# One weight load placed between the two halves of the first k and v loads, and its rounding done there

## The chip, the cores and the metric

The kernel runs on one core of one Trainium2 chip. The metric is the device time in microseconds of that core, the median of several executions. Before the change four executions took 1024.33 to 1025.48 us, with a median of 1025.05 us.

## The reference

The program is an attention without softmax, followed by a gated feed-forward block on its output.

```python
kv = np.einsum('bhsd,bhse->bhde', k, v)          # 8 batches, 8 heads, 576 x 64
out = np.einsum('bhsd,bhde->bhse', q, kv)
rms = np.sqrt(np.mean(out * out, axis=-1, keepdims=True) + 1e-06)
x = (out / rms * g_norm)                         # then (B,H,S,D) -> (B*S, H*D) = 4608 x 512
g = x @ w_gate                                   # 512 x 1536
silu = g * (1.0 / (1.0 + np.exp(-g)))
return (silu * (x @ w_val) @ w_out).astype(np.float32)
```

q, k, v and g_norm are float32. The three weight matrices are float64, so that each element is two 32-bit words; the kernel makes float32 values of them on the chip.

## The kernel before, in words

**Blocks.** The 4608 tokens are cut into nine blocks of 512. Each block has an attention part (class `Att`) and a feed-forward part (class `Ffn`). Block 0 is treated apart: its feed-forward part multiplies plainly, as soon as each weight piece is there (`plain_up`, L1009 to L1024), while later blocks use products with fewer multiplications (`Up`, `Inner`, `Down`). The change touches only what happens before and during block 0's `plain_up`.

**Start of block 0.** Four statements at L1060 to L1063 issue the loads: the first half of q (two transfers of 256 KB), k and v (`load_first_kv`), the second half of q, and the first four weight pieces. `load_first_kv` goes through two groups of four heads; each group has a large transfer of k and one of v on SyncE's queue (L230, 512 KB each) and a small one of each on ScalarE's queue (L233, 64 KB each). `first` then does the attention of block 0:

- `turn_q(0)` transposes q's first half on TensorE (L335), and ScalarE and VectorE copy the result out (L337, L339).
- `first_kv` multiplies k by v (L248): 36 small matmuls for the heads of the first group, and 36 for those of the second. ScalarE copies one bank (L252) and VectorE adds the other (L253, shown as its helper L111).
- `product` multiplies q by that (L355), squares on ScalarE (L366) and sums on VectorE (L367). It is done for both halves, with `turn_q(1)` between.
- `warm` issues seven 128x512 matmuls whose result nobody reads (L482).
- `root` and `scale` compute the reciprocal root and multiply (L373 to L392, the multiplication shown as helper L113); `turn_x` transposes the result (L402) and copies it into `x` on ScalarE (L403).

**Weight pieces.** There are 36 pieces of 512 KB, in the order w_gate 0, w_val 0, w_gate 1, ... and then w_out. Each is loaded into one of four `ld` buffers (L135), which q's two halves use too, and rounded by `Words`. `begin` (L139) is an Abs on ScalarE (L146) and three operations on VectorE (L147, L152, L153). `finish` (L157) is one activation on ScalarE (L160) and an addition on VectorE that writes the weight (L162). A ring of five buffers `r` holds the intermediate values, and q's and the attention's too.

**What sets the order.** The instructions are put on the engines' queues by a scheduler; `tc.issue_after` keeps an instruction from being placed before another. Each engine then works through its own queue in order. `weights(n)` (L1046) loads four pieces ahead and rounds up to piece n. In `first`, piece 0 is begun after the second half of q is copied (L466), between the two products, and finished after the scaling (L473). `weights(2)` follows at L1072, and then two pieces more for each step of `plain_up`.

Of the kernel before, what the change touches and what calls it, by code (L numbers as in the profile page):

```python
# [18 lines left out]
def kernel(  # L19
# [154 lines left out]
    words = {}  # L174

    def load_w(name, j):
        src = wviews[name][1]
        if name == "o":
            words[name, j] = Words(src[:, j : j + 1, :], (1,))
        else:  # L180
            words[name, j] = Words(src[:, :, 2 * P * j : 2 * P * (j + 1)], (NS,))

    def round_w(name, j):
        if name == "o":
            dst = wo[:, j : j + 1, :]
        else:
            dst = wviews[name][0][j // 2][:, :, P * (j % 2) : P * (j % 2 + 1)]
        piece = words.pop((name, j))
        if not piece.begun:
            piece.begin()  # L190
        return piece.finish(dst)

    class Att:
# [12 lines left out]
        def parts(self, t):  # L206

            n, first = self.n, P * t - D * self.n
            if t < self.cut:
                return [(n - 1, S + first, 0, P)]  # L210
            if t == self.cut and self.split:
                return [(n - 1, S - D, 0, D), (n, 0, D, P)]
            return [(n, first, 0, P)]
# [7 lines left out]
        def load_first_kv(self):  # L221


            room = self.room.rearrange("p f (h x) -> p (f h) x", h=2)
            most = {"k": room[:, 0:H], "v": room[:, H : 2 * H]}
            last = {x: room[:, 2 * H + i].rearrange("p (h d) -> p h d", d=D) for i, x in enumerate("kv")}
            for g in range(2):
                heads, rows = slice(NS * g, NS * (g + 1)), slice(D * g, D * (g + 1))
                for x, src in (("k", k), ("v", v)):
                    nc.sync.dma_start(  # L230
                        out=most[x][:, heads], in_=src[0, heads, 0:BLK].rearrange("h (p t) d -> p h (t d)", t=T)
                    )
                    nc.scalar.dma_start(out=last[x][rows], in_=src[0, heads, BLK:S].rearrange("h p d -> p h d"))  # L233
            self.k, self.v = (
                [most[x].rearrange("p h (t d) -> p h t d", t=T)[:, :, t] for t in range(T)] + [last[x]] for x in "kv"
            )
# [220 lines left out]

        def first(self):
            self.turn_q(0, (b_psum, c_psum))
            self.first_kv()  # L460
            self.product(0)
            with tc.issue_after(self.multiplied.ins):
                self.turn_q(1, (b_psum, c_psum))

            with tc.issue_after(self.copied_q.ins), tc.issue_after(self.summed.ins):
                begun = words[pieces[0]].begin()  # L466
            with tc.issue_after(begun.ins):
                self.product(1, (b_psum, a_psum))
            self.warm()
            self.root(0, 2)  # L470
            self.scale(0)
            with tc.issue_after(self.squared.ins), tc.issue_after(self.scaled.ins):
                weights(1)  # L473
            self.turn_x(0)
            self.scale(1)
            return self.squared, self.scaled
# [557 lines left out]
    pieces = [(x, j) for j in range(NF) for x in "gv"] + [("o", j) for j in range(NF)]  # L1034
# [3 lines left out]
    def load_weights(upto):  # L1038
        nonlocal loaded, sent
        while loaded < min(upto, len(pieces)):  # L1040
            load_w(*pieces[loaded])
            loaded += 1
            if loaded == len(pieces) - NP:
                sent = words[pieces[loaded - 1]].sent

    def weights(upto):  # L1046
        nonlocal rounded
        while rounded < min(upto, len(pieces)):
            load_weights(rounded + 4)
            round_w(*pieces[rounded])  # L1050
            rounded += 1

    def t2(place, b22, b11):

        sub(nc.vector, place, b22, place)
        add(nc.vector, place, place, b11)

    blocks = [Att(n) for n in range(NB)]
# [7 lines left out]
    for n in range(NB):  # L1066
        ffn = Ffn(n, blocks[n])
        nxt = blocks[n + 1] if n + 1 < NB else None
        if n == 0:

            with tc.issue_after(squared.ins), tc.issue_after(scaled.ins):
                weights(2)  # L1072
            ffn.plain_up(0, (0,))
            copied = blocks[0].copied
            blocks[0].turn_x(1)
            for f in range(NF):
                with tc.issue_after(blocks[0].copied.ins if f else copied.ins):
                    weights(2 * (f + 2))
                ffn.plain_up(f) if f else ffn.plain_up(0, (1,))
            weights(len(pieces))  # L1080
            pairs = wo.rearrange("p (j e) d -> p e j d", e=2)
            t2(pairs[:, 0, :, HD:DM], pairs[:, 1, :, HD:DM], pairs[:, 0, :, 0:HD])
            nxt.room = x_pool.tile([P, 3, 7, P], F32, name="xi").rearrange("p a b c -> p (a b c)")

            with tc.issue_after(sent.ins):
                for i in range(2):
                    nxt.load_kv(i)
                for i in range(2):
                    nxt.load_q(i)
            ffn.plain_end()  # L1090
            for g in range(2):
                nxt.kv(g)
        else:

            def third():
                nxt.kv(0)
                nxt.load_kv(1)

            def two_thirds():
                nxt.kv(1)  # L1100
                if nxt.n == 2:
                    for i in range(2):
                        nxt.load_q(i)

            fill = {4: third, 8: two_thirds} if nxt else {}
            if n == DEEP:
                for a, at in enumerate((1, 2, 3, 5)):
                    fill[at] = lambda i=a // 2, j=a % 2: nxt.load_quarters(i, (j,))
            ffn.up(fill)
        if nxt:  # L1110
            nxt.turn()
        if 0 < n < NB - 2:
            blocks[n + 2].load_kv(0)
        if DEEP <= n < NB - 2:
            for i in range(2):
                blocks[n + 2].load_q(i)
        ffn.down(nxt)
        if n == 0:
            blocks[2].load_kv(0)

            with tc.issue_after(nxt.halves[0].ins):
                for j in range(NP // 2):
                    t2(wv[j][:, 0:2], wv[j][:, 2:4], wg[j][:, 0:2])
            with tc.issue_after(ffn.down_.s4.ins):
                for j in range(NP // 2, NP):
                    t2(wv[j][:, 0:2], wv[j][:, 2:4], wg[j][:, 0:2])
# [31 lines left out]
```

## Time and profile before

| | |
|---|---|
| median of four runs | 1025.05 us (1024.33 to 1025.48) |
| profiled execution: its own time, its span | 1026.5 us, 1024.7 us |
| TensorE, VectorE, ScalarE, GpSimd busy, share of the span | 98%, 68%, 22%, 36% |
| mean transfer rate over the span; in the first 25.6 us | 166 GB/s; 216 GB/s |
| second half of the k-by-v products begins | 14.84 us |
| first full-width multiplication of the feed-forward part begins | 39.96 us |

The page lists the busy time of each engine, then the span in 40 slices of 25.6 us with the busy share of each in tenths. The chain of work that ended last is followed back from the last instruction: at each step to what released it, or to the instruction before it on its engine. In the timeline a row has the start, the length, the engine, the line, the operation, the tiles written and read, the shapes and how many instructions are merged; behind it, in brackets, the idle time of the engine just before and what ended it. SPq and ACTq are the queues that issue transfers. A transfer's length in the chain runs from its issue to its landing. A matmul of float32 values is recorded as two instructions, a transpose as one.

### The profile page before, as it was taken

The page shows a single profiled execution, that of the slowest core. Times are in us where ns is not written, and L with a number is a line of the kernel's source. Part 1 is how long each engine was busy: PE and PEld are TensorE (multiplying, and loading weights), DVE is VectorE, ACT ScalarE, POOL GpSimd, SP SyncE. Part 2 cuts the span into 40 slices and gives each one's busy share as a digit, 9 for nine tenths or more (in the row PEclk, how much of TensorE's full clock was granted, in tenths as well). Part 3 has the DMA queues.
Part 4 walks back from the last instruction along what each step waited for, and adds up shares of the span by engine and source line. Part 5 has one row for each costly group of instructions (what it writes and reads, how often), then busy time and mean ns, then how long its engine had stood idle before and what let it go on. Part 6 is the DMA issues. An engine that isn't in the chain of part 4 may idle for free.

```text
span 1024.7 us, 21404 instructions
## 1 busy us (share of the span) xinstructions
PE 1007.8 (98%) x8522; PEld 898.2 (88%) x8522; DVE 701.3 (68%) x1168; ACT 227.9 (22%) x352; POOL 368.9 (36%) x280
## 2 busy tenths in 40 slices
PE   5999999999999999999999999999999999999998
PEld 4544688888999989998999899988998999989997
DVE  2999688998666855685657566665669466956661
ACT  2666111221111212221121111111112111211110
POOL 0000263434045512561246314730555046413670
PEclk9999999999999999999999999999999999999999
DMA  7689644667888467845686468637762766066601
GB/s 216 198 256 268 122 82 128 170 153 173 243 224 239 79 154 207 253 102 116 212 240 151 83 203 244 186 56 199 231 195 54 177 196 187 21 164 207 190 28 42
DMA packets 273844, 170.26 MB, mean 166 GB/s; under 512 B 150608, under 2 KB 241872, under 8 KB 273744
## 3 DMA queue, kind: packets, MB, share of 16 engines
q1 hardware_dynamic: 238800, 164.42, 58.6%
q10 hardware_dynamic: 34880, 4.46, 2.7%
q8 instruction: 68, 1.11, 0.4%
q14 instruction: 32, 0.26, 0.1%
q0 software_dynamic: 64, 0.00, 0.0%
HBM read 138.02 MB, written 22.41 MB: 157 GB/s over the span
## 4 chain that ended last, share of the span: by engine, by line
PE 91%; DVE 5%; DMA 2%; issue 1%; ACT 1%; SPq 0%; DVEq 0%; ACTq 0%
PE b L714 26%; PE b L551 19%; PE c L714 13%; PE c L551 10%; PE a L714 6%; PE a L551 5%; PE b L1018 4%; PE c L1018 4%; PE m L314 2%; PE m L355 1%; DVE r L112 1%; DVE xi L112 1%; DMA h<-in_v_dram 1%; DVE r L111 1%; DVE t L112 1%
## 5 line engine op out<-in xcount | busy, mean ns | idle before, releaser
L111 POOL TENSOR_TENSOR r<-r 128x256 f32<-128x256 f32 (+1 forms) x105 | 110.8, 1061 | 301.1 <-DVE r L111 272.4
L111 DVE TENSOR_TENSOR r<-b,r 128x512 f32<-128x512 f32 (+1 forms) x273 | 162.0, 606 | 65.6 <-PE b L714 60.6
L112 POOL TENSOR_TENSOR t<-wo 128x512 f32<-128x512 f32 x81 | 114.4, 1436 | 214.9 <-DVE wo L111 105.8
L111 DVE TENSOR_TENSOR r<-c,r 128x512 f32<-128x512 f32 (+1 forms) x179 | 108.5, 617 | 87.9 <-PE c L714 54.5
L714 PE MATMUL b<-x,t 128*128 128x128 f32 x1092 | 151.2, 275 | 0.0
L111 DVE TENSOR_TENSOR r<-a,r 128x512 f32<-128x512 f32 (+1 forms) x99 | 62.5, 631 | 113.5 <-PE a L551 71.1
L714 PEld LDWEIGHTS b<-x,t 128*128 128x128 f32 x1092 | 136.5, 192 | 0.8 <-DVE r L111 0.2
L714 PE MATMUL c<-xi,t 128*128 128x128 f32 x840 | 112.4, 275 | 0.4 <-DVE xi L111 0.4
L113 POOL TENSOR_TENSOR h<-r 128x1024 f32<-128x1024 f32 (+1 forms) x40 | 82.2, 2068 | 78.1 <-DVE r L111 75.0
L714 PEld LDWEIGHTS c<-xi,t 128*128 128x128 f32 x840 | 102.9, 192 | 0.5 <-DVE xi L111 0.5
L551 PE MATMUL b<-wo,h 128*128 128x256 f32 x432 | 100.1, 383 | 0.1
L551 PE MATMUL b<-t,h 128*128 128x256 f32 x432 | 96.9, 381 | 0.0
L551 PEld LDWEIGHTS b<-t,h 128*128 128x128 f32 x432 | 81.5, 190 | 11.4 <-issue 0.2
L551 PEld LDWEIGHTS b<-wo,h 128*128 128x128 f32 x432 | 79.8, 190 | 13.2 <-DVE h L113 2.5
L728 ACT COPY r<-b 128x512 f32<-128x512 f32 x63 | 36.9, 586 | 211.5 <-PE b L714 211.5
L714 PE MATMUL b<-xi,t 128*128 128x128 f32 x588 | 79.7, 276 | 0.0
L714 PEld LDWEIGHTS b<-xi,t 128*128 128x128 f32 x588 | 72.4, 192 | 0.0
L714 PE MATMUL b<-x,wg 128*128 128x128 f32 x336 | 52.7, 279 | 0.2 <-DVE x L112 0.2
L714 PE MATMUL b<-x,wv 128*128 128x128 f32 x336 | 51.3, 275 | 0.0
L551 PE MATMUL a<-wo,h 128*128 128x256 f32 x216 | 48.3, 379 | 0.0
L551 PE MATMUL c<-t,s 128*128 128x256 f32 x216 | 48.1, 379 | 0.0
L551 PE MATMUL c<-wo,h 128*128 128x256 f32 x216 | 48.1, 379 | 0.0
(128 smaller groups left out, 1564.8 us busy)
## 6 DMA issues: line engine op xcount, KB each, us to landing
t<-w SPq DMA_DIRECT2D x336, 256.0 KB, 3.4
out_dram<-r SPq DMA_DIRECT2D x17, 512.0 KB, 3.1
ld<-in_k_dram SPq DMA_DIRECT2D x26, 288.0 KB, 4.9
ld<-in_v_dram SPq DMA_DIRECT2D x26, 288.0 KB, 5.9
ld<-in_moe_w_gate_dram SPq DMA_DIRECT2D x12, 512.0 KB, 4.8
ld<-in_moe_w_val_dram SPq DMA_DIRECT2D x12, 512.0 KB, 4.7
ld<-in_moe_w_out_dram SPq DMA_DIRECT2D x12, 512.0 KB, 4.9
w<-t SPq DMA_DIRECT2D x18, 256.0 KB, 3.3
```

The lines of the kernel that those rows point to most:

```text
L111: add = lambda e, o, a, b: e.tensor_tensor(out=o, in0=a, in1=b, op=OP.add)
L112: sub = lambda e, o, a, b: e.tensor_tensor(out=o, in0=a, in1=b, op=OP.subtract)
L113: mul = lambda e, o, a, b: e.tensor_tensor(out=o, in0=a, in1=b, op=OP.mult)
L314: nc.tensor.matmul(self.kv_ps[r][u * D : (u + 1) * D, g, :], lhsT=k[:, u, c, :], rhs=v[:, u, c, :], start=(c == 0), stop=(c == KT - 1),)
L355: self.multiplied = nc.tensor.matmul(self.ps[i][u][p : p + D, t, j, :], lhsT=self.qt[rows, 2 * i + t, j, p : p + D], rhs=kvs[b % 3][rows, ...
L551: nc.tensor.matmul(banks[e][:, e], lhsT=lhsT, rhs=rhs, start=first and i == 0 and (e == 0 or banks[0] is not banks[1]), stop=i == self.ste ...
L714: nc.tensor.matmul(ps[:, i, f], lhsT=self.weight(o, p, f), rhs=self.operand(o, p), start=first and (i, f) == (0, 0), stop=True, skip_group ...
L728: nc.scalar.copy(out=dst, in_=ps)
L1018: nc.tensor.matmul(t, lhsT=w[f // 2][:, i, P * (f % 2) : P * (f % 2 + 1)], rhs=x[:, i, of], start=(i == 0), stop=(i == NS - 1),)
```

## The change

The load of piece 0 (w_gate 0) is issued within `load_first_kv`, behind k and v of the first group of heads and ahead of those of the second; `load_weights(1)` has an effect only the first time that the loop reaches it. Piece 0 is rounded whole between `turn_q(0)` and `first_kv`. Where piece 0 was begun, piece 1 (w_val 0) is begun now, and each later call of `weights` reaches one piece further. The condition in `weights` asks whether q's second half has been asked for; it has been at every call.

```diff
@@ load_first_kv @@
                     nc.scalar.dma_start(out=last[x][rows], in_=src[0, heads, BLK:S].rearrange("h p d -> p h d"))
+                load_weights(1)
@@ first @@
             self.turn_q(0, (b_psum, c_psum))
+            weights(1)
             self.first_kv()
...
-                begun = words[pieces[0]].begin()
+                begun = words[pieces[1]].begin()
...
             with tc.issue_after(self.squared.ins), tc.issue_after(self.scaled.ins):
-                weights(1)
+                weights(2)
@@ weights @@
-            load_weights(rounded + 4)
+            load_weights(rounded + 4 if blocks[0].q[2:] else 1)
@@ block 0 @@
             with tc.issue_after(squared.ins), tc.issue_after(scaled.ins):
-                weights(2)
+                weights(3)
```

In the instructions as built, SyncE's queue differs from before in the place of this one load (it stands behind k and v of the first heads) and in two neighbouring transfers near 90 us. On TensorE the order differs only at the start of the feed-forward part. Before, it is: four matmuls with w_gate, seven transposes, four matmuls with w_val, one transpose. After, it is: one matmul with w_gate, four with w_val, four transposes, three with w_gate, four transposes. ScalarE's and VectorE's orders differ until all pieces are rounded, and are the same from then on. The load of w_val 1 takes the buffer that piece 0 has left, where before it took that of q's second half.

## Prediction

> **What bounds the kernel now.** I read the busy shares first, then the chain that ended last for the first 45 us, then the queue of SyncE and the other engines over the same stretch. From the page:
>
> ```profile
> PE 1007.8 (98%) x8522; PEld 898.2 (88%) x8522; DVE 701.3 (68%) x1168; ACT 227.9 (22%) x352; POOL 368.9 (36%) x280
> PE   5999999999999999999999999999999999999998
> ```
>
> TensorE is busy in all but the first slice of 25.6 us. So an edit at the start is worth what it does to the moment from which TensorE runs without a gap. The chain that ended last, in order of time (start, length, what):
>
> ```profile
> 5.22 9.48 DMA h<-in_v_dram
> 14.84 2.44 PE m L248 x72
> 17.37 0.43 DVE kv L111
> 17.85 1.99 PE m L355 x64
> ...
> 33.52 1.28 ACT L1023
> 34.81 0.39 ACT h L1023
> 35.20 0.57 ACT r L160
> 35.77 0.59 ACT x L403
> 36.36 0.04 issue
> 36.41 1.99 PE b L1018 x8
> 38.40 1.73 PE c L1018 x8
> 40.13 3.43 PE b L1018 x8
> ```
>
> Until 14.70 us the end hangs on a transfer, v of the second four heads. From 14.84 to 30 us it hangs on TensorE and the work of block 0's attention; from 31 to 36.4 on ScalarE; from 36.41 on TensorE alone: the chain holds nothing but L1018 from there to 115.66. What moves the start of the first full-width L1018 group, 39.96 us, moves the end; what lies beside that path costs nothing. The queues at the start, from the timeline (start, length, engine, operation):
>
> ```profile
> 4.81 0.37 SPq L230 DMA_DIRECT2D h<-in_k_dram  x1
> 5.22 1.14 SPq L230 DMA_DIRECT2D h<-in_v_dram  x1
> 6.46 5.13 SPq L298 DMA_DIRECT2D ld<-in_q_dram  x2
> 11.63 2.72 SPq L135 DMA_DIRECT2D ld<-in_moe_w_gate_dram  x1
> 11.75 2.40 PE L248 MATMUL m<-h 64*64 64x64 f32 x72 [4.69 <-DMA h<-in_v_dram]
> 14.84 2.41 PE L248 MATMUL m<-h 64*64 64x64 f32 x72 [0.69 <-DMA h<-in_v_dram]
> ...
> 31.26 1.99 PE L1018 MATMUL b<-x,wg 128*128 128x256 f32 x8 [0.34 <-ACT x L403]
> 33.09 0.69 DVE L162 CUSTOM_DVE_ANT_0 wv<-r 128x1024 uint16<-128x1024 uint16 x1
> 33.85 1.97 PE L1018 MATMUL c<-x,wv 128*128 128x256 f32 x8
> ```
>
> Both halves of L248 wait for v, the first until 11.75, the second until 14.84. The transfer queue is full in that time. The stretches' row (TensorE's, its loads', VectorE's, ScalarE's, GpSimd's busy time, clock, share of the 16 transfer engines, GB/s):
>
> ```profile
> 6.00:12.00 6.00, 1.31 (x13) 0.94 (x17) 0.23 (x1) 0.59 (x1) 0.00 (x0) 1.00 1.09 325
> ```
>
> **The change part by part.** Times below are those of the profiled execution: span 1024.7 us, its own time 1026.5 us, against a median of 1025.05 us of the four runs. I work out a difference from the profiled run and add it to the median.
>
> *The load, moved.* One issue of 512 KB goes on SP from behind k, v and the two q loads to a place ahead of k and v of the second heads: past four issues (k, v, q, q). The issue took 0.37 to 2.72 us of SP; at the new place SP is free at 4.81, so k is issued at about 5.2 instead of 4.81, v at about 6.5 instead of 5.22. Both still stand behind 1 MB that lands by 11.75, so issue time is not the price. The price is 512 KB ahead of k and v in a queue that serves in order. The two L248 groups give it: 1 MB (k and v of the second heads) between 11.75 and 14.84, 3.09 us, so 1.54 us per 512 KB. Other rows: 512 KB at 325 GB/s is 1.61 us; at the 216 GB/s that the page gives for the whole first slice it is 2.43 us. Nothing would be the lower end, if the transfer engines had room; their share of 1.09 in 6 to 12 us speaks against it. I take 1.54, the row of the same packets at the same place, and keep 0 and 2.43 for the range.
>
> DMA: Bandwidth & Descriptors (the Trainium skill), section Specifications, gives a limit of about 358 GB/s per core from HBM; 512 KB by it would be an estimated 1.46 us and the sum 0.08 us smaller. Its Rules for kernel authors say to issue a DMA early and wait on it late; here early means in front of transfers that the chain waits for, and the trace's rows decide against that rule.
>
> *What waits behind k and v.* L248's second half, the sum L111, the product L355, the q transposes, the second product, the warming L482, the root and scale: all of it moves by 1.54 us, since each hangs on the one before. q's second half stays behind v in the queue and lands 1.54 us after its new v at the latest as now; L335 at 19.77 started with no wait, and it moves too.
>
> *The first piece's rounding, moved.* On ScalarE the Abs (L146, 0.68 us) and the unit (L160, 0.67 us) now stand before and after the copy of the second q tile; on VectorE L152, L147, L153 and L162 (0.42, 0.43, 0.69, 0.68 us) stand before the sum L111. The Abs waits for the weight, about 11.75 + 1.54 = 13.3 us. Queued behind it on ScalarE: the q copy (at 7.10 now, needed by L355 at 19.4) and the kv copy (18.4); on VectorE: L111 at 18.9. ScalarE would be through at about 15.3, VectorE at 16.3. Cost nothing; the cover is the wait for k and v, and without it (weight landing with v at 16.2) VectorE would end near 18.9, still hardly late.
>
> *The begin at 22.25, replaced.* The Abs, the three VectorE operations and the L160 that stood there for piece 0 now stand there for piece 1 (w_val), same kinds and sizes. Piece 1 has the same bytes ahead of it as piece 0 and 1 had together; the transfer share falls to 0.15 by 20 to 21 us, so it is in by then, against a need at 22.25 + 1.54 = 23.8. Nothing.
>
> *The gap before 36.41.* With piece 1 finished at 30.0 (the L162 at 29.35) instead of 33.8, the order of TensorE changes: one matmul on wg, four on wv, four transposes, three on wg, four transposes, then the second half. ScalarE's order was L146, L160, L146, table load, Silu, L160, two copies of x (L403); it becomes L146, L160, copy, table load, Silu, copy. That is 1.7 us of rounding less to 0.57 + 0.58, but a copy that must wait for transposes stands ahead of the table load (1.28). Replayed without the shift: a matmul is two records, spaced 0.216 us at 256 columns; a transpose takes 0.109. The first wg matmul runs 31.26 to 31.79, the four on wv to 33.52, four transposes to 33.96 (the last result 0.2 later), their copy 34.16 to 34.84, the table load to 36.12, the Silu to about 36.4, the other copy to 37.09. TensorE's three wg matmuls and four transposes end at 35.69; the next half starts there, does two matmuls, waits from 36.55 to 37.15 for the other copy, and its wv part starts at 38.01 instead of 38.24. Gain 0.22 us. Bounds: 0, and TensorE's whole idle time between 29.88 and 39.96: 10.08 less 16 x 0.109 less 32 x 0.216 = 1.42 us. I take 0.22.
>
> *The fourth weight (w_val, second piece).* Its issue waited until 21.76 for L335 to free a q buffer; now it takes the buffer of piece 0 and goes out some 6 us earlier. It stands behind everything the chain needs. Later loads, and VectorE's order of roundings to 104.5 us, shift among themselves; L1018 has no wait for a weight in 36 to 115 us. Nothing, cover: the lead of the rounding, L162 of the piece for 43.40 ends at 37.9.
>
> *TensorE's clock.* Four 128-wide transposes took 1.11 us at 19.77 and eight took 1.04 at 29.88: the array doubles its speed between. The first warming half-step took 0.72 us, the next 0.43. If the doubling keeps its distance to the work, nothing; if it keeps its time, L482 gains 0.29; if it comes late, L482 at half speed (14 x 0.43 more) is the far bound, 6.0. I take 0, as nothing in the busy stretch from 17.85 on changes but its start.
>
> TensorE: Matmul & The Clock Gate (the Trainium skill), section Part 1, says that the full clock is granted after a busy window of about 3.4 us of a free-running count. Being a window late would make that an estimated 1.7 us at most; the added idle time of L248 (14.15 to 16.4) is shorter than a window.
>
> **Sum.** 1.54 - 0.22 = +1.3 us: 1026.4 us on the median, 1027.8 by the profiled run's own time. That is 0.13%, under the 0.2% (2.05 us) that I take as what a measurement of this kernel can tell from no change.
>
> **The rivals.**
> - *The transfer costs more.* At 216 GB/s it is 2.43, and the sum +2.2: 1027.3, slower by over 0.2%; it decides from a price of 2.27 us on. For it: the slice's mean, and the q packets that halve the rate to 193 GB/s in 12 to 16 us. Against: these lie behind v.
> - *The clock comes late.* L248's longer idle time and the shifted work delay the doubling. Each us more of half speed in L482 costs 0.5 us, and nothing hides it: L402 follows L482 (30.04), the scale is ready before (29.43). With 2 us of delay the sum is +2.3: 1027.4; from 1.5 us on it decides. For it: the doubling lies within 1 us of L482's start.
> - *The load hides.* k and v are not delayed, the gap closes: -0.2 to -1.4, 1023.6 to 1024.8, and with 0.6 from an earlier clock (30.04 down to the scale's 29.43) it just reaches 2 us. Against: the full queue.
> - *The weight does not go ahead*, so that only order changes: +-0.2. The changed kernel's order of instructions on SP rules it out, where the load stands fourth.
>
> **How the numbers follow.** Forecast (own range 1025.6 to 1027.1) 0.50; dear transfer 0.25; late clock 0.13; hidden load 0.12, half of it over 0.2%. Slower: 0.25 + 0.13 and 0.03 of the forecast's edge. Same: the rest of the forecast with half the hidden load. For 8 in 10 the range leaves out half of each end: 1024.4 to 1028.2, the upper end being dear transfer with half of a late clock.
>
> **What would show it.** In the changed kernel's profile: L248's second half starting at 16.4 (at 17.3 the transfer was dear; at 14.8 hidden); the Abs at about 13.3; L482 ending at 31.6; the table load ahead of the first full-width L1018, which starts at 41.3. The prediction is wrong if that start is not 1.3 us later, or if it is and the end is not: then a later stage gave or took time.

## The result, and the profile after

The changed kernel takes 1026.7 us (median of 30 runs, 1025.21 to 1028.92); the kernel before, run beside it, takes 1024.95 us (median of 48 runs, 1023.63 to 1026.22). The ratio is 1.0018, with a 95% interval of 1.0012 to 1.0023. That is +1.75 us, within +1.2 and +2.4: slower by an amount that the interval separates from zero. The middle value is just inside the 0.2% that the prediction counts as no change, the upper end of the interval is not. The forecast was +1.3 us on a median of 1025.05, so 1026.4 us.

The profiled executions differ by less than the medians: span 1024.7 us before, 1025.0 us after. The profiled execution before lies above its own median (1026.5 us against 1024.95), that of after on its own (1026.73 against 1026.7). So the difference of the two spans is not the effect of the change, and everything below is read as distances within one execution.

The page of the changed kernel, busy shares:

```profile
PE 1006.6 (98%) x8522; PEld 897.3 (88%) x8522; DVE 702.3 (69%) x1168; ACT 227.9 (22%) x352; POOL 368.8 (36%) x280
...
PE   5999999999999999999999999999999999999998
```

Hardly anything has changed there: TensorE still works without a gap after the first slice. So the first 41 us are compared, as in the prediction. The changed file has one more line from L234 on and two more from about L462 on, so L249, L336, L356, L403, L484 and L1020 below are what was L248, L335, L355, L402, L482 and L1018.

The timeline of the changed kernel at the start (start us, us, engine, line, operation, number merged, and in brackets the idle time before with what ended it):

```profile
4.51 0.37 SPq L135 DMA_DIRECT2D ld<-in_moe_w_gate_dram  x1
4.92 0.89 SPq L230 DMA_DIRECT2D h<-in_k_dram  x1
...
11.09 2.40 PE L249 MATMUL m<-h 64*64 64x64 f32 x72 [4.32 <-DMA h<-in_v_dram]
...
12.62 0.68 ACT L146 ACTIVATE r<-ld 128x512 f32<-128x512 f32 x1 [7.77 <-DMA ld<-in_moe_w_gate_dram]
...
14.64 0.69 DVE L162 CUSTOM_DVE_ANT_0 wg<-r 128x1024 uint16<-128x1024 uint16 x1
...
15.80 2.42 PE L249 MATMUL m<-h 64*64 64x64 f32 x72 [2.31 <-DMA h<-in_v_dram]
...
21.64 0.68 PE L336 MATMUL c<-ident,ld 128*128 128x128 f32 x4
```

The weight's issue now stands ahead of k and v of the second heads. The two groups of small products start 4.71 us apart (11.09 and 15.80), where they were 3.09 us apart, and the second waits 2.31 us for v instead of 0.69. The rounding of the weight (the Abs at 12.62, the last step at 14.64) is done before the second group starts. The transfer engines were as full as before in this time, and the rate was no higher:

```profile
6.00:12.00 6.00, 1.68 (x37) 1.30 (x37) 0.00 (x0) 0.00 (x0) 0.00 (x0) 1.00 1.06 316
```

The same timeline at the start of the feed-forward part:

```profile
30.27 1.06 PE L403 MATMUL m<-ident,r 128*128 128x128 f32 x8 [0.28 <-DVE r L113]
31.68 0.70 PE L1020 MATMUL b<-x,wg 128*128 128x256 f32 x2 [0.34 <-ACT x L404]
...
35.28 1.28 ACT L1025 ACT_TABLE_LOAD   x1
...
36.58 0.38 ACT L1025 ACTIVATE h<-b 128x256 f32<-128x256 f32 x1
36.86 0.68 ACT L404 ACTIVATE x<-m,gain 128x512 f32<-128x512 f32 x1
...
37.01 1.99 PE L1020 MATMUL b<-x,wg 128*128 128x256 f32 x8 [0.49 <-ACT h L1025]
...
40.57 3.60 PE L1020 MATMUL b<-x,wg 128*128 128x512 f32 x8
```

The same places before (the second four transposes, L402, and the first full-width groups with wg and with wv):

```profile
20.68 1.06 PE L335 MATMUL c<-ident,ld 128*128 128x128 f32 x4
...
29.88 1.04 PE L402 MATMUL m<-ident,r 128*128 128x128 f32 x8
...
39.96 3.60 PE L1018 MATMUL b<-x,wg 128*128 128x512 f32 x8
43.40 3.60 PE L1018 MATMUL c<-x,wv 128*128 128x512 f32 x8
```

The order of TensorE is the one that the built program showed. The second copy of x (L404 at 36.86) stands behind the table load and the Silu. From the first matmul on wg to the first full-width group it took 8.89 us (31.68 to 40.57), against 8.70 before. The second half on wg stood still for 0.49 us until the Silu (L1025) had read the first half.

**The sum of one execution.** The table gives distances in us; all but the last column are from the timelines. "g" are the starts of the two groups of small products, "q" the start of the product L355, "T" that of the transposes L402, "b" the first matmul with wg, "f" the first full-width group. The last column is how long after "q" TensorE's speed doubled, from the trace's record of its clock, which begins with the doubling (at 24.00 us before, at 21.79 after). Four of the experiments of the next section stand in it too.

| kernel | first g at | g to g | second g to q | q to T | T to b | b to f | first g to f | doubling after q |
|---|---|---|---|---|---|---|---|---|
| before | 11.75 | 3.09 | 3.01 | 12.03 | 1.38 | 8.70 | 28.21 | 6.15 |
| after | 11.09 | 4.71 | 3.01 | 11.46 | 1.41 | 8.89 | 29.48 | 2.98 |
| load alone | 11.84 | 4.79 | 3.02 | 12.02 | 1.38 | 8.71 | 29.92 | 6.13 |
| load behind | 10.52 | 3.02 | 3.02 | 12.08 | 1.37 | 8.90 | 28.39 | 6.24 |
| two loads | 10.98 | 6.28 | 3.01 | 11.73 | 1.40 | 8.90 | 31.32 | 4.06 |
| own bank | 11.90 | 4.68 | 3.02 | 11.83 | 1.38 | 8.61 | 29.52 | 5.65 |

After less before: +1.62 for the load, +0.03, +0.19 in the gap, and -0.57 between q and T: together +1.27 from the first group on. The first group itself started 0.66 us earlier, which gives the +0.61 by which the first full-width group is late (40.57 against 39.96). The last term and that earlier start are not the change's as far as these runs tell. The start of the first group lies between 10.52 and 11.90 us in these six profiles, with no order by kernel. The -0.57 is TensorE's clock: in the execution after, the second four transposes took 0.68 us (last line of the first timeline above), where they took 1.06 us in the other five. The whole distance q to T lies between 11.46 and 12.08 us in the six, and in all six the later the doubling, the longer it is. (The granted clock in the rows of the stretches is no help here: it reads 1.00 throughout this stage in all six, also ahead of the doubling.) Without those two, the load and the gap make +1.84 us with the 0.03, and the medians differ by 1.75.

Between the first full-width group and the end, the delay in this pair of executions goes from +0.61 to +0.23 us at the last matmul, most of it in one stretch at 224 to 243 us. From the start of that group to the start of the last matmul it is 981.06 us before and 980.68 after; with the load alone 980.25, with the load behind 981.12, with two loads 980.78, with the own bank 980.43, and 980.72 in the kernel before with early matmuls, which leaves the load where it was. The seven lie within 0.87 us, and two loads have no gain at 224 to 243 us. So nothing in these profiles lays this difference to the change, and no later stage adds to the loss.

### The profile page after: what moved, and what is told of

Its sections match the earlier page's. It is cut to its first block, busy times and chain, and to the rows that moved or that the text cites. A ratio compares the mean times of both kernels' runs of the same rounds, so it can differ in the third digit from the quotient of the medians.

```text
span 1025.0 us, 21403 instructions
## 1 busy us (share of the span) xinstructions
PE 1006.6 (98%) x8522; PEld 897.3 (88%) x8522; DVE 702.3 (69%) x1168; ACT 227.9 (22%) x352; POOL 368.8 (36%) x280
## 4 chain that ended last, share of the span: by engine, by line
PE 84%; DVE 9%; DMA 4%; SPq 1%; issue 1%; ACT 1%; ACTq 0%; DVEq 0%
PE b L716 26%; PE b L553 20%; PE c L716 13%; PE c L553 10%; PE a L716 6%; PE a L553 5%; DVE r L153 1%; PE m L356 1%; DMA h<-in_v_dram 1%; PE m L315 1%; SPq L283 1%; DVE xi L112 1%; DVE r L147 1%; DMA ld<-in_moe_w_out_dram 1%; DVE r L152 1%
## 5 line engine op out<-in xcount | busy, mean ns | idle before, releaser
L113 POOL TENSOR_TENSOR h<-r 128x1024 f32<-128x1024 f32 (+1 forms) x40 | 81.9, 2064 | 78.5 <-DVE r L111 75.0
```

Of the source, the lines that this page charges most:

```text
L113: mul = lambda e, o, a, b: e.tensor_tensor(out=o, in0=a, in1=b, op=OP.mult)
```

## The experiments

The theory: the 512 KB ahead of k and v cost their own transfer time on the path, some 1.6 us, and the new order in front of the second half costs 0.2 us more, because of the Silu. The rivals: the loss comes from the rounding that now stands between `turn_q(0)` and `first_kv`; it comes from a clock that doubles later; or it lies in a later stage.

### The load alone

Before, with the load moved and no rounding moved.

```diff
                     nc.scalar.dma_start(out=last[x][rows], in_=src[0, heads, BLK:S].rearrange("h p d -> p h d"))
+                load_weights(1)
```

> Only the load of piece 0 is moved, between the two groups of k and v; the rounding and every other order stay as before. If the queue is the cause, the second L248 group starts 4.6 to 4.8 us after the first (3.09 before) and the time is +1.5 to +1.7 us, about as much as the whole change (+1.75). If the cause is the new order of the rounding (the second half of the first feed-forward step waits for the Silu), the load alone is worth 0 to +0.5 us.

Measured: 1026.44 us (11 runs, 1025.54 to 1027.51) against 1024.98 us for before; ratio 1.0017 (1.0008 to 1.0026), so +1.46 us. Its timeline:

```profile
11.84 2.40 PE L249 MATMUL m<-h 64*64 64x64 f32 x72 [4.91 <-DMA h<-in_v_dram]
16.63 2.42 PE L249 MATMUL m<-h 64*64 64x64 f32 x72 [2.40 <-DMA h<-in_v_dram]
...
31.67 1.04 PE L403 MATMUL m<-ident,r 128*128 128x128 f32 x8
33.05 1.99 PE L1019 MATMUL b<-x,wg 128*128 128x256 f32 x8 [0.34 <-ACT x L404]
...
41.76 3.60 PE L1019 MATMUL b<-x,wg 128*128 128x512 f32 x8
```

The groups stand 4.79 us apart, 1.70 more than before, and every later distance is that of before within 0.01 us, the gap (8.71) among them. So the load alone makes nearly all of the loss, and the moved rounding is not needed for it. The distance is as expected; the time is just under the +1.5 to +1.7 us.

### The load behind k and v

The changed kernel with the load issued behind k and v of both groups and ahead of q's second half, and the rounding after `first_kv`.

```diff
@@ load_first_kv @@
-                load_weights(1)
+            load_weights(1)
@@ first @@
-            weights(1)
             self.first_kv()
+            with tc.issue_after(self.copied_kv.ins), tc.issue_after(self.added_kv.ins):
+                weights(1)
```

> The load stands behind both groups of k and v and ahead of q's second half, the rounding of piece 0 follows the sum of the k-by-v banks; everything behind is ordered as in the changed kernel. If the queue is the cause, the groups of L248 are 3.1 us apart again and the time is within -0.5 to +0.4 us of before. If the new order costs, it stays at +1.0 us or more.

Measured: 1025.50 us (11 runs, 1024.29 to 1027.0); ratio 1.0006 (0.9997 to 1.0015), +0.5 us, not told apart from no change. That is 0.1 us above the expected range, and the interval reaches to +1.5 us, so the time alone does not rule out the other expectation, +1.0 us or more. The distances do:

```profile
10.52 2.40 PE L249 MATMUL m<-h 64*64 64x64 f32 x72 [3.45 <-DMA h<-in_v_dram]
13.54 2.41 PE L249 MATMUL m<-h 64*64 64x64 f32 x72 [0.63 <-DMA h<-in_v_dram]
...
35.35 1.99 PE L1021 MATMUL b<-x,wg 128*128 128x256 f32 x8 [0.74 <-ACT h L1026]
```

The groups are 3.02 us apart again, the second group to q is 3.02 us as before, and the first group to the first full-width group 28.39 us against 28.21. The piece is still rounded early, and it brings no gain: the distance b to f is 8.90, as in the changed kernel, with a wait for the Silu again (0.74 us). So, together with the load alone, the place of the load made the loss, and not the early rounding.

### Two loads between

```diff
-                load_weights(1)
+                load_weights(2)
```

> The changed kernel with two weight pieces between the groups instead of one. If the queue is the cause, the groups are 6.2 to 6.4 us apart and the time is +3.0 to +3.6 us against before. If the transfer engines had room, or the order is the cause, it stays at about +1.8 us.

Measured: 1028.47 us (5 runs, 1027.25 to 1028.73); ratio 1.0033 (1.0020 to 1.0045), +3.5 us, as expected if the queue is the cause.

```profile
10.98 2.40 PE L249 MATMUL m<-h 64*64 64x64 f32 x72 [4.31 <-DMA h<-in_v_dram]
17.26 2.41 PE L249 MATMUL m<-h 64*64 64x64 f32 x72 [3.88 <-DMA h<-in_v_dram]
```

The groups are 6.28 us apart: 3.19 more than before for two loads, 1.60 each. No load, one load and two loads lie nearly on one line, 1.6 us per 512 KB. That is 328 GB/s, close to the rate at which the transfer engines ran in this stretch (305 to 325 GB/s in the rows of 6 to 12 us of the six kernels).

### A bank of its own for the second half

The changed kernel; the wg result of plain_up's second half goes to a new tile of the `b` ring, where it shared a tile with the first half that the Silu reads.

```diff
             if 0 in halves:
                 self.ps[f] = [pool.tile([P, 2, HB], F32, name=pool.name[0]) for pool in (b_psum, c_psum)]
+            elif f == 0:
+                self.ps[f][0] = b_psum.tile([P, 2, HB], F32, name="b")
```

> The changed kernel, but the second half of the first feed-forward step writes w_gate's product into a bank of its own, which the Silu of the first half doesn't read. If the wait for the Silu holds that half back, it now starts right behind the four transposes, waits for the second copy of x in its middle, and the step after it starts 0.3 to 0.4 us earlier counted from the first L1018: -0.3 us against the changed kernel. If the copy of x holds it, nothing moves.

Measured: 1026.80 us (11 runs, 1025.9 to 1027.85); ratio 1.0018 (1.0010 to 1.0027).

```profile
37.41 1.03 PE L1022 MATMUL b<-x,wg 128*128 128x256 f32 x4
37.71 0.38 ACT L1027 ACTIVATE h<-b 128x256 f32<-128x256 f32 x1
...
38.72 1.13 PE L1022 MATMUL b<-x,wg 128*128 128x256 f32 x4 [0.29 <-ACT x L404]
...
41.42 3.60 PE L1022 MATMUL b<-x,wg 128*128 128x512 f32 x8
```

The second half now starts at 37.41, before the Silu at 37.71, and then waits for the copy of x, as the prediction had replayed it. The distance b to f falls from 8.89 to 8.61 us, just under the expected 0.3 to 0.4. So the Silu's hold on the shared tile is what kept the gap from closing. In the median this 0.28 us doesn't show; it is less than these runs can tell.

### An earlier clock

A test of the clock's part, on the kernel before: four 128x512 matmuls whose result nobody reads, between `turn_q(0)` and `first_kv`. They are extra work and leave nothing out.

```diff
             self.turn_q(0, (b_psum, c_psum))
+            self.early(4)
...
+        def early(self, count):
+            ps = a_psum.tile([P, NS, P], F32, name="a")
+            for _ in range(count):
+                nc.tensor.matmul(ps, lhsT=ident, rhs=self.q[0], start=True, stop=True)
```

> The kernel before, with four more 128x512 matmuls that nobody reads between the transposes of q's first half and the k-by-v products, where TensorE waits for v. If the time to the first feed-forward step depends on when the array's speed doubles, the transposes of q's second half take 0.11 us each instead of 0.21 and the second product 1.1 us instead of 1.9, the scaling is ready near 26.6 us instead of 29.4, and the time is -2 to -3 us against before. If the wait for k and v alone sets it, -0.3 to +0.5 us.

Measured: 1027.02 us (10 runs, 1025.41 to 1028.12) against 1024.98; ratio 1.0021 (1.0011 to 1.0030), 2.0 us slower. The expectation was missed, sign included. The timeline of TensorE:

```profile
7.98 4.34 PE L483 MATMUL a<-ld,ident 128*128 128x512 f32 x7
12.25 1.38 PE L248 MATMUL m<-h 64*64 64x64 f32 x72
14.53 1.40 PE L248 MATMUL m<-h 64*64 64x64 f32 x72 [0.90 <-DMA h<-in_v_dram]
16.66 1.15 PE L355 MATMUL m<-kv,r 64*64 64x64 f32 x61 [0.73 <-DVE kv L111]
20.33 0.33 PE L355 MATMUL m<-kv,r 64*64 64x64 f32 x3 [2.53 <-issue]
20.59 1.12 PE L335 MATMUL b<-ident,ld 128*128 128x128 f32 x4
```

The clock did double early: each group took 1.38 to 1.40 us instead of 2.40. But in the middle of the next product TensorE stood still for 2.53 us and waited for nothing that the profile shows ("issue"). The stretches' rows (the last three columns are the granted clock, the share of the transfer engines and GB/s) show what that cost further:

```profile
18.00:19.00 1.00, 0.00 (x0) 0.00 (x0) 0.00 (x0) 0.00 (x0) 0.00 (x0) 1.00 1.00 335
...
21.00:22.00 1.00, 1.00 (x7) 1.00 (x6) 0.25 (x1) 0.72 (x2) 0.00 (x0) 0.50 0.06 16
...
24.00:25.00 1.00, 1.00 (x22) 0.66 (x15) 0.97 (x3) 0.63 (x2) 0.00 (x0) 1.00 0.93 302
```

The clock fell back to half from about 20.6 to 24 us, so that the transposes L335 and the second product ran slowly again. L335 began at 20.59, where it began at 19.77 before, although the second group had started 0.31 us sooner. The first full-width group is 0.87 us later than before if counted from the second group (25.99 against 25.12), so about 1.2 of the 2.0 us is not located by this profile. What held TensorE is not settled. It stopped behind the 61st of the product's 64 recorded matmuls, and at the same place, for 1.67 us, in the next kernel, with the same early matmuls. The transfer engines were full in the first half of the stall. The trace has a packet of 16 KB of the queue that the profile's page calls "instruction" in transfer at that time: from 18.12 to 19.09 us here (stall 17.81 to 20.33), from 16.11 to 17.32 in the next kernel (stall 17.14 to 18.81). That TensorE's own instructions came late would fit, but no run took it apart.

### Everything together

The changed kernel with the load behind k and v, the bank of its own, the four early matmuls, piece 1 begun only after the second product, and five warming matmuls instead of seven: an attempt at a version that beats both. The parts that have not been shown yet:

```diff
-            with tc.issue_after(self.copied_q.ins), tc.issue_after(self.summed.ins):
-                begun = words[pieces[1]].begin()
-            with tc.issue_after(begun.ins):
-                self.product(1, (b_psum, a_psum))
+            self.product(1, (b_psum, a_psum))
...
-            for _ in range(7):
+            for _ in range(5):
```

> The early matmuls; the load of piece 0 behind both groups of k and v, its rounding behind the sum of the banks; no begin of piece 1 ahead of the second product; five warming matmuls instead of seven; w_gate's second half in a bank of its own. The begin took 1.4 us of VectorE between the two sums of squares, so the scaling should be ready near 25.3 us: -3 to -4.3 us against before. If the begin was hidden behind TensorE, no better than the early matmuls alone.

Measured: 1024.75 us (11 runs, 1023.66 to 1025.97) against 1024.98; ratio 0.9998 (0.9989 to 1.0006). The expectation was missed. L403 began at 28.38, 1.50 us before that of the kernel before. The first full-width group with wg (40.18) is no mark here, because one of its four matmuls now runs ahead of wv's second half. The first full-width group with wv begins at 42.75, where it began at 43.40 before; counted from the second group of small products that is 28.88 us against 28.56, so nothing was won on the path.

The single runs show one more thing. In seven of the eleven, the profiled one among them, the mean granted clock was 0.996 to 0.998, and they took 1024.41 to 1025.97 us; the profile has the clock at half speed from 20.4 to 23.8 us. In the other four it was 1.00, and they took 1023.66 to 1023.93 us, all below the fastest of the 26 runs of the kernel before (1024.14). In the experiment ahead of this one, too, the one run at 1.00 was the fastest of the ten (1025.41). So the fallen clock goes with the longer times. This is a sorting of runs after the fact; no run made the clock stay up.

### The same without the early matmuls

The last kernel without `early(4)`.

> The same without the early matmuls. -1.0 to -1.8 us against before if VectorE's 1.4 us and the two warming matmuls were on the path; about 0 if the late doubling of the array's speed takes it back.

Measured: 1025.14 us (11 runs, 1024.42 to 1025.73); ratio 1.0003 (0.9994 to 1.0012). Missed too. The rows of TensorE and ScalarE in its timeline:

```profile
28.57 1.06 PE L403 MATMUL m<-ident,r 128*128 128x128 f32 x8 [1.41 <-DVE r L113]
29.97 0.70 PE L1020 MATMUL b<-x,wg 128*128 128x256 f32 x2 [0.34 <-ACT x L404]
...
36.32 1.28 ACT L1025 ACT_TABLE_LOAD   x1
...
38.51 1.99 PE L1020 MATMUL c<-x,wv 128*128 128x256 f32 x8 [0.71 <-DVE h L113]
40.34 2.74 PE L1020 MATMUL b<-x,wg 128*128 128x512 f32 x6
42.91 3.60 PE L1020 MATMUL c<-x,wv 128*128 128x512 f32 x8
```

and of VectorE:

```profile
27.13 1.29 DVE L113 TENSOR_TENSOR r<-m,y 128x512 f32<-128x512 f32 x2
28.33 0.42 DVE L147 TENSOR_SCALAR r<-r 128x512 f32<-128x512 f32 x1
...
30.80 0.68 DVE L162 CUSTOM_DVE_ANT_0 wv<-r 128x1024 uint16<-128x1024 uint16 x1
```

With fewer warming matmuls L403 no longer hangs on TensorE but on VectorE's scaling (1.41 us of waiting). And VectorE, freed of piece 1's begin before the scaling, now does it between the parts of the scaling, so that w_val is there only at 31.48 (30.80 and 0.68), and the table load comes 6.35 us after the first matmul with wg, where it came 3.60 us after it in the changed kernel. The second half on wv then waits 0.71 us, until VectorE (L113) has multiplied the Silu's result with the first half of wv's tile: the own bank is for wg alone, and wv's two halves still share a tile. Counted from the second group, L403 begins 0.87 us earlier than before (14.17 us against 15.04), to which an earlier doubling (4.39 us after q) may add; but from the first matmul with wg to the first full-width group with wv it takes 12.94 us against 12.14, which takes that back. (The distance b to f, 10.37 us, overstates it, as the row with 6 instead of 8 records at 40.34 shows.) So over all their runs neither kernel is faster than before by an amount that these runs can tell.

## Why the prediction was right, point by point

**The load, +1.54.** Right in mechanism and nearly in size. The distance of the two groups grew by 1.62 us in the changed kernel, 1.70 with the load alone and 1.60 per load with two, and not at all with the load behind k and v (-0.07). The row that gave 1.54, 1 MB in 3.09 us, was 4 to 10% too fast for the 512 KB in front of it; the rate of the stretch, which gave 1.61, was closer. The estimate of 1.46 us, which the prediction works out from a page's limit, was further off, 9 to 14% under the measured 1.60 to 1.70. The upper bound of 2.43 from the first slice's mean is excluded, and so is the lower bound, no cost at all.

**What waits behind k and v.** Right: the second group to q stayed at 3.01 to 3.02 us in all six profiles, and with the load alone everything up to the first full-width group moved as one.

**The first piece's rounding, 0.** Right. The Abs began at 12.62 us where 13.3 was predicted; the first group was 0.66 us earlier in this execution, which accounts for it. The load behind k and v, which rounds later, beside the product, shows no cost in the distances, and the load alone has the loss without the moved rounding.

**The begin at 22.25, replaced, 0.** Not against the evidence, but its cover was thinner than the text says: in the profiled execution after, the clock was early, TensorE's warming matmuls ended before VectorE, and the chain that ended last went through piece 1's begin:

```profile
22.57 1.18 DVE z L368 x2
23.75 0.34 DVE r L147
24.09 0.34 DVE r L152
24.46 0.69 DVE r L153
...
28.84 1.30 DVE r L113 x2
...
30.27 0.64 PE m L403 x4
```

L403 waited 0.28 us for the scaling there. Before, the same steps of piece 0 stood at this place, so it costs nothing against before; but it caps what an earlier clock can give.

**The gap before the second half, -0.22.** This is the step that failed. The predicted order of TensorE came out, and so did ScalarE's. But the replay let the second half start as soon as TensorE was through with the transposes, 4.43 us after the first matmul with wg (35.69 less 31.26). It started 5.33 us after it (37.01 less 31.68), because its matmul writes the tile whose first half the Silu was still to read. Before, the copy of x came later than the Silu and hid that wait (0.48 us for L403 at 36.41). The term measured +0.19 instead of -0.22. With a tile of its own it was -0.09: the wait for the copy of x came where the replay had it, and the rest of the 0.13 is small distances between instructions.

**The clock, 0.** In the median nothing more is needed: the load and the gap make +1.8, and +1.75 was measured. In single executions it is not zero. The distance q to T varied by 0.62 us in six profiles, one each of different kernels, so that a part that belongs to the change can't be told from chance. The first marker of the prediction that depends on it, the warming matmuls ending at 31.6, came out with the load alone (L403 begins at 31.67) and not in the changed kernel's profile (L403 begins at 30.27, after 0.28 us of waiting).

*TensorE: Matmul & The Clock Gate* (the Trainium skill), section Part 1, says that the activity window is free-running, so that the moment of the doubling varies from run to run. The spread of the doubling, 2.98 to 6.24 us after q, agrees with that; no kernel was profiled twice, so no run here shows it for one kernel. The busy window of about 3.4 us that the prediction takes from the same section is not what these profiles show for the small products: the doubling came 6.0 to 9.3 us after the second group began, though TensorE stood still for 0.60 us at most on the way.

**The sum.** +1.3 predicted, +1.75 measured (+1.2 to +2.4). The two terms miss by +0.08 and +0.41, which is the whole difference within its interval. The load's term carried the forecast; the other had the wrong sign, and was only small. The prediction's own test, the first full-width group at 41.3, 1.3 us late, was not met in the profile after: it began at 40.57, +0.61. Counted from the first group it is +1.27, but that it comes so near the forecast is chance, since -0.57 of it is the clock of that execution. Of the rivals, the dear transfer and the hidden load are excluded by the distances of the groups; the late clock is not seen in the changed kernel, where it was early; and the weight did go ahead.

## What to carry to other kernels

Here a load put in front of a load that the critical path waits for cost its own transfer time in full, with the transfer engines busy: 1.6 to 1.7 us for each 512 KB, and its early arrival brought nothing. To find what the new order of an engine is worth, replay it with every reader of a shared tile, not only with the engines' own queues: a wait that was hidden behind a later one appears when the later one goes. A difference of single profiles of this kernel is uncertain by about as much as the effect, so read distances within one execution and let the medians confirm their sum.

## What was not expected of the hardware

The start of the first group of small products, which waits for a transfer, lay between 10.52 and 11.90 us in six executions whose instructions up to there were nearly the same. TensorE at full clock stopped for 2.53 us (1.67 us in the kernel with everything together) for no reason that the profile names, and its clock was at half speed again some 2.8 us after the stop began (17.81 to about 20.6), for 3.4 us in both kernels. With the early matmuls the transposes L335 began 0.8 us later (20.59 against 19.77) and the kernel was 2.0 us slower.
